# Joining C and V in one transpose, diagonal blocks of old states, and a new order of the tensor engine's groups in a chunked linear-attention kernel with a routed MLP behind it

## The chip, the cores and the metric

The kernel runs on one core of one Trainium2 chip. The metric is the device time of one execution in microseconds (us). Profiles and traces come from the hardware profiler on that core; in them PE is the tensor engine's matmuls, PEld its weight loads, DVE the vector engine, ACT the scalar engine, POOL GpSimd and SP the engine that issues most of the transfers. "Ln" is line n of the kernel.

## The reference

Two blocks, one behind the other. The first runs, for each of 4 x 8 heads, a 40 x 40 state over 768 time steps; the second sends each token to one of eight experts (by a hash of its id) and applies a two-layer MLP.

```python
def _attn_ref(r, k, v, w, a, b):              # all (4, 8, 768, 40)
    state = zeros((B, H, D, D))
    for t in range(S):
        y[:, :, t] = einsum('bhd,bhde->bhe', rt, state)       # read with the state before t
        Sa = einsum('bhde,bhe->bhd', state, at)
        state = state * wt[:, :, None, :] - einsum('bhd,bhe->bhde', Sa, bt)
        state = state + einsum('bhd,bhe->bhde', vt, kt)
    return y

def _moe_ref(x, token_ids, w1, w2):           # x = y as (3072, 320)
    expert_idx = token_ids * 2654435761 % 8
    for e in range(8):
        xe = x[expert_idx == e]
        out[expert_idx == e] = maximum(xe @ w1[e], 0) @ w2[e]  # 320 -> 1024 -> 320
```

Everything is float32. The change touches the first block alone.

## The kernel before

The time axis is cut into 12 chunks of C = 64 steps; D = 40, R = C + D = 104. A **tile** u is one chunk of two of the four batches (NG = 2 groups of batches), so there are 24 tiles of 16 heads. A head is named by `be` (batch of the two), `hp` (pair of heads, 0..3) and `par` (which head of the pair); `al = hp // 2`, `hq = hp % 2`. A pair's two heads lie in columns 0..39 and 64..103 of a 104-wide row; after a transpose they lie in partitions 0..39 and 64..103, which is what `half40(par)` selects.

The work is written as steps, each with a time in **ticks**; the program sorts all steps by that time and emits them in that order, so each engine runs them in that order. Tile u has its transposes of `at` and `z` and its scores `a` in tick u, and its recurrent part in tick u + 8. A tick thus holds the first part of one tile and the recurrent part of the one eight before it: ticks 0 to 7 have only first parts, ticks 24 to 32 only recurrent parts. Within a tick the order is that of `STEPS`:

```python
    psa = apool("psa", 2, space=bass.MemoryType.PSUM)      # single banks: bank(...)
    psb = apool("psb", 3, space=bass.MemoryType.PSUM)      # pairs of banks: two_banks(...)
    st_r = ring("st", NG, [R, 2, HP, D], all_of)           # states
    sd_r = ring("sd", NG, [R, 2, HP, D], all_of)           # old states, transposed
    ...
    STEPS = ["r1", "v_t", "at_t", "c", "z", "x", "y", "r_t", "sd", "s", "a", "r0", "u", "rc"]
```

The recurrent part of tile u, with t0 = u + 8 (`mm` is one matmul, `heads_by` yields the heads in the order named):

```python
        @at_tick(t0 - 1, "v_t")                        # V transposed, half the partitions at a time
        def _():
            p = two_banks("v_ps")
            for hp in range(HP):
                for be in range(2):
                    rows = half(1 - be)
                    nc.tensor.transpose(p[0:R, be, hp * C:(hp + 1) * C], x["x"][rows, be, hp, 0:R], ident[rows, rows])
            nc.scalar.copy(t[0:R].rearrange("p b h t -> p b (h t)"), p[0:R, :, 0:HP * C])

        @at_tick(t0 - 1, "r0")                         # r1, part from the state: a matmul per head
        def _():
            x["r1_ps"] = p = two_banks("r1_ps")
            for par, be, hp in heads_by("hq", "be", "al", "par"):
                c0 = (hp % HQ * 2 + be) * D
                mm(p[half(al(hp)), par, c0:c0 + D], x["at_t"][half40(par), hp, be, :], st[half40(par), be, hp, :], ...)

        @at_tick(t0, "r1")                             # r1, part from V; 8 matmuls, then a copy
        ...
        @at_tick(t0, "c")                              # C (for the state) and C transposed (for the scores)
        def _():
            p = two_banks("c_ps")
            for par, be, hp in heads_by("hq", "be", "al", "par"):
                mm(p[half(par), a, c0:c0 + C], r1[half(a), par, hp % HQ * 2 + be, :], um[half(a), h, :])
            if not last:
                q = two_banks("nc_ps")
                for par, be, hp in heads_by("hq", "par", "al", "be"):
                    mm(q[half(be), a, c0:c0 + D], um[half(a), h, :], r1[half(a), par, hp % HQ * 2 + be, 0:D])
            nc.scalar.copy(ct[:]..., p...)             # c_t
            ...                                        # two copies of q into x["x"], beside V

        @at_tick(t0, "rc")                             # scores of r: with C and with V, a matmul each
        def _():
            p = two_banks("rc_ps")
            for i in range(2):
                for par, be, hp in heads_by("hq", "al", "be", "par"):
                    c0 = (hp * 2 + be) * C
                    mm(p[half(be ^ i), par, c0:c0 + C], x["v_t" if i else "c_t"][half40(par), be, hp, :],
                       x["r_t"][half40(par), hp, be, :])
            nc.vector.tensor_tensor(mr..., p..., after..., op=OP.mult)      # mask, 128 x 1024

            @at_tick(t0, "s")                          # new state
            def _():
                p = bank([P, 2, HP * D], "s_ps")
                mm(p[0:R], ident[0:R, 0:R], flat, stop=False)               # the old state, 320 columns
                for par, be, hp in heads_by("be", "al", "hq", "par"):
                    mm(p[half40(par), be, hp * D:(hp + 1) * D], x["z"][:, be, hp, cols], x["x"][:, be, hp, cols], ...)
                for be in range(2):                    # times the decay of the chunk, 104 x 160 each
                    nc.vector.tensor_tensor(st[:, be], p[0:R, be]..., pend, op=OP.mult)

        @at_tick(t0 + 1, "y")                          # output rows: r times old state, scores times z
        def _():
            p = two_banks("y_ps")
            for par, be, hp in heads_by("al", "hq", "be", "par"):
                mm(p[half(be), par, hp * D:(hp + 1) * D], x["r_t"][half40(par), hp, be, :], sd[half40(par), be, hp, :], ...)
            for par, be, hp in heads_by("al", "hq", "par", "be"):
                mm(p[half(be), par, hp * D:(hp + 1) * D], x["mr"][:, par, hp * 2 + be, :], x["z"][...], start=False)
            nc.vector.tensor_tensor(by_parity(xs), p..., by_parity(x["py"]), op=OP.mult)

            @at_tick(t0 + 1, "sd")                     # 8 transposes of the state, two copies of 40 x 320
```

Beside these, a tick holds the transposes `at_t` (4), `z` (8) and `r_t` (4), the scores `a` (32 matmuls), and the steps `x` and `u` (16 matmuls each, 32 x 32 x 32) that finish a 64 x 64 triangular inverse; groups of four tiles have 32-step inverses on the vector engine (`outer`, `ub`), and six rounds of running products of the decays w lie there too (`pb`, `qb`). Behind the last tick comes the MLP.

Of the kernel before, what the change touches and what calls it, by code (L numbers as in the profile page):

```python
# [33 lines left out]
F32 = mybir.dt.float32  # L34
# [9 lines left out]
def kernel(  # L44
# [102 lines left out]
    psa = apool("psa", 2, space=bass.MemoryType.PSUM)  # L147
    psb = apool("psb", 3, space=bass.MemoryType.PSUM)
# [31 lines left out]
    st_r = ring("st", NG, [R, 2, HP, D], all_of)  # L180
    sd_r = ring("sd", NG, [R, 2, HP, D], all_of)
# [51 lines left out]
    def heads_by(*order):  # L233

        sizes = {"par": 2, "be": 2, "al": 2, "hq": HQ}
        idx = [{}]
        for o in order:
            idx = [{**d, o: i} for d in idx for i in range(sizes[o])]
        for d in idx:
            yield d["par"], d.get("be"), d["al"] * HQ + d["hq"]  # L240
# [37 lines left out]
    STEPS = ["r1", "v_t", "at_t", "c", "z", "x", "y", "r_t", "sd", "s", "a", "r0", "u", "rc"]  # L278
# [111 lines left out]
    def tile_a(u):  # L390
# [20 lines left out]
        @at_tick(u - 0.5)  # L411
# [25 lines left out]
        def _():  # L437
            gi, ti = divmod(u, GRP)
            p = two_banks("a_ps")
            for kb in range(2):  # L440
                order = ("hq", "al", "be", "par") if kb == 0 else ("hq", "be", "al", "par")
                for par, be, hp in heads_by(*order):

                    i, c0 = (1 - be, hp * C) if kb == 0 else (al(hp), (HP + be * HQ + hp % HQ) * C)
                    mm(p[half(i), par, c0:c0 + C], x["z_t"][half40(par), be, hp, half(be if kb else 1 - be)],
                       x["at_t"][half40(par), hp, be, :])
# [65 lines left out]
    def tile_m(u, t0):  # L512
# [6 lines left out]
        def _():  # L519
# [3 lines left out]
            for par, be, hp in heads_by(*x_order):  # L523
# [10 lines left out]
        def _():  # L534
            ug, xi = groups[gi]["ug"][:, ti * H:(ti + 1) * H, :], x["xi"]
            p = bank([P, H, BLK], "u_ps")
            for par, be, hp in heads_by(*x_order):
# [5 lines left out]
    def tile_s(u, t0):  # L543
# [24 lines left out]
        @at_tick(t0 - 1, "v_t")  # L568
        def _():
            x["v_t"] = t = work.tile([P, 2, HP, C], F32, tag="v_t", name="v_t")  # L570
            p = two_banks("v_ps")
            for hp in range(HP):
                for be in range(2):
                    rows = half(1 - be)
                    nc.tensor.transpose(p[0:R, be, hp * C:(hp + 1) * C], x["x"][rows, be, hp, 0:R], ident[rows, rows])
            nc.scalar.copy(t[0:R].rearrange("p b h t -> p b (h t)"), p[0:R, :, 0:HP * C])

    def tile_b(u, t0):
# [6 lines left out]
        def _():  # L585
            x["r1_ps"] = p = two_banks("r1_ps")
            for par, be, hp in heads_by("hq", "be", "al", "par"):
                c0 = (hp % HQ * 2 + be) * D
                mm(p[half(al(hp)), par, c0:c0 + D], x["at_t"][half40(par), hp, be, :], st[half40(par), be, hp, :],
                   start=be == 0 and hp % HQ == 0, stop=False)  # L590

        @at_tick(t0, "r1")
        def _():
            p = x.pop("r1_ps")

            for par, _, hp in heads_by("hq", "par", "al"):
                c0 = hp % HQ * 2 * D
                mm(p[half(al(hp)), par, c0:c0 + 2 * D], x["mk"][:, par, hp, :], x["x"][:, :, hp, par * C:par * C + D],
                   start=False)
            x["r1"] = r1 = r1_r(u)  # L600
            nc.scalar.copy(r1[:, :, :, 0:D], p[:, :, 0:HP * D].rearrange("p two (x e) -> p two x e", e=D))

        @at_tick(t0, "c")
        def _():

            r1, um = x["r1"], x["um"]
            p = two_banks("c_ps")
            for par, be, hp in heads_by("hq", "be", "al", "par"):
                h, a = hx(par, be, hp), al(hp)
                c0 = (be * HQ + hp % HQ) * C  # L610
                mm(p[half(par), a, c0:c0 + C], r1[half(a), par, hp % HQ * 2 + be, :], um[half(a), h, :])
            if not last:
                q = two_banks("nc_ps")
                for par, be, hp in heads_by("hq", "par", "al", "be"):
                    h, a = hx(par, be, hp), al(hp)
                    c0 = (hp % HQ * 2 + par) * D
                    mm(q[half(be), a, c0:c0 + D], um[half(a), h, :], r1[half(a), par, hp % HQ * 2 + be, 0:D])
            x["c_t"] = ct = work.tile([P, 2, HP, C], F32, tag="c_t", name="c_t", bufs=1)
            nc.scalar.copy(ct[:].rearrange("p b (a q) t -> p a b (q t)", a=2),
                           p[:, :, 0:HP * C].rearrange("p a (b x) -> p a b x", b=2))  # L620
            if not last:
                for be in range(2):
                    nc.scalar.copy(x["x"][half(be), be].rearrange("p (a q) (two e) -> p a (q two) e", a=2, two=2)[:, :, :, 0:D],
                                   q[half(be), :, 0:HP * D].rearrange("p a (x e) -> p a x e", e=D))

        @at_tick(t0, "rc")
        def _():
            p = two_banks("rc_ps")
            for i in range(2):
                for par, be, hp in heads_by("hq", "al", "be", "par"):  # L630

                    c0 = (hp * 2 + be) * C
                    mm(p[half(be ^ i), par, c0:c0 + C], x["v_t" if i else "c_t"][half40(par), be, hp, :],
                       x["r_t"][half40(par), hp, be, :])
# [5 lines left out]
        if not last:  # L640
            @at_tick(t0, "s")
            def _():
                p = bank([P, 2, HP * D], "s_ps")
                flat = st[:].rearrange("p b h e -> p b (h e)")
                mm(p[0:R], ident[0:R, 0:R], flat, stop=False)
                for par, be, hp in heads_by("be", "al", "hq", "par"):
# [5 lines left out]
                for be in range(2):  # L652
                    pend = pend_r(ri)[:, :, rn, 2 * g + be].unsqueeze(2).to_broadcast([R, HP, D])
# [451 lines left out]
```

## Time and profile before

| | us |
|---|---|
| median of three runs | 780.6 (779.1 to 787.19) |
| span of the profiled execution | 790.1 |
| PE / PEld / DVE / ACT / POOL busy | 640.8 / 473.6 / 375.8 / 267.2 / 227.9 |
| scores of r masked (`mr`) of the first / last tile start at | 145.48 / 504.90 |

Busy time of an engine is the sum of its instructions' spans. On PE these overlap in the pipeline and end by a model, so the time of a group of matmuls is better read as the distance between the starts of that group and of the next. Every float32 matmul stands in the trace as two records (two pairs of a weight load and a matmul), every transpose as one. The 24 starts of `mr` cut the attention block into tiles: one per tick. A timeline line has start, length, engine, line, operation, output tile and input tiles, sizes (partitions x columns of the weights, then partitions x elements of the output), how many instructions were merged, and in brackets the idle time of the engine before it and what ended it; "issue" there means that nothing in the trace explains the wait.

### The profile page before, as it was taken

The numbers are of one execution on the slowest core, as the hardware profiler recorded it, in microseconds if no ns is written. First come the engines' busy times: TensorE is split into PE (matmuls) and PEld (weight loads), VectorE is DVE, ScalarE is ACT, GpSimd is POOL, SyncE is SP. The second block draws the span as 40 slices with busy tenths as digits, with TensorE's granted clock in tenths as the row PEclk, the third lists the DMA queues.
The fourth block names the chain that finished last, engine by engine and source line by source line (L and its number), as shares of the span: only waits on it lengthen the run. The fifth ranks groups of instructions, "written<-read, shape, count | busy, mean of one in ns | idle before, by whom it ended". The sixth has DMA issues, their size and how long they took to land.

```text
span 790.1 us, 25829 instructions
## 1 busy us (share of the span) xinstructions
PE 640.8 (81%) x11272; PEld 473.6 (60%) x11272; DVE 375.8 (48%) x925; ACT 267.2 (34%) x598; POOL 227.9 (29%) x383
## 2 busy tenths in 40 slices
PE   0055558888888888787888989679999999999995
PEld 0044446767777777676777877536555565564653
DVE  8155999956765887455647733222202022020210
ACT  0023335534454555364554545200213032100110
POOL 3223214313253633433341312161231312312101
PEclk9999999957887988789897979869999999999998
DMA  4979884864698688586252332382435327323000
GB/s 89 176 134 168 145 140 102 158 121 80 90 144 132 107 130 136 80 162 97 37 70 64 69 78 54 75 280 89 139 101 159 100 92 249 84 84 101 25 9 19
DMA packets 205686, 86.35 MB, mean 109 GB/s; under 512 B 186687, under 2 KB 196160, under 8 KB 205569
## 3 DMA queue, kind: packets, MB, share of 16 engines
q1 hardware_dynamic: 193408, 47.60, 33.1%
q0 software_dynamic: 12160, 37.06, 19.0%
q8 instruction: 89, 1.46, 0.8%
q14 instruction: 29, 0.23, 0.1%
HBM read 68.85 MB, written 16.42 MB: 108 GB/s over the span
## 4 chain that ended last, share of the span: by engine, by line
PE 50%; issue 24%; DVE 12%; DMA 4%; POOL 4%; SPq 3%; ACT 1%; POOLq 0%; DVEq 0%; another core or an unknown queue 0%
PE y_ps L252 6%; PE up_ps L887 6%; PE dn_ps L905 5%; PE s_ps L252 4%; PE t_ps L467 4%; PE r_ps L252 4%; PE rc_ps L252 3%; PE z_ps L432 3%; PE sd_ps L683 3%; PE x_ps L252 2%; DMA qb<-in_w_dram 2%; PE c_ps L252 2%; PE a_ps L252 2%; POOL out_dram L910 2%; PE nc_ps L252 2%
## 5 line engine op out<-in xcount | busy, mean ns | idle before, releaser
L895 DVE TENSOR_SCALAR ht<-up_ps 128x448 f32<-128x448 f32 x32 | 20.0, 625 | 196.4 <-PE up_ps L892 130.5
L905 PE MATMUL dn_ps<-w,ht 128*128 128x320 f32 (+1 forms) x448 | 109.5, 433 | 0.0
L905 PEld LDWEIGHTS dn_ps<-w,ht 128*128 128x128 f32 (+1 forms) x448 | 72.0, 177 | 32.1 <-issue 1.3
L887 PE MATMUL up_ps<-xt,w 128*128 128x448 f32 x224 | 87.5, 544 | 0.0
L910 POOL DMA_INDIRECT out_dram<-o,idx_all x28 | 27.6, 986 | 196.4 <-ACT o L909 191.4
L675 POOL DMA_DIRECT2D x_rows<-xs x44 | 23.3, 535 | 200.0 <-DVE xs L669 163.2
L887 PEld LDWEIGHTS up_ps<-xt,w 128*128 128x128 f32 x224 | 41.7, 190 | 43.1 <-issue 37.9
L501 DVE TENSOR_TENSOR ub<-ub,outer 128x31 f32<-128x31 f32 (+15 forms) x186 | 63.8, 343 | 6.4
L498 DVE TENSOR_TENSOR outer<-ub,nb 128x31 f32<-128x31 f32 (+15 forms) x186 | 63.0, 339 | 4.8
L897 ACT ACTIVATE ht<-up_ps 128x448 f32<-128x448 f32 x32 | 17.4, 543 | 130.5 <-PE up_ps L892 102.2
L909 ACT COPY o<-dn_ps 128x320 f32<-128x320 f32 x28 | 11.9, 425 | 103.3 <-PE dn_ps L905 103.3
L404 POOL DMA_DIRECT2D pl<-p_rows x48 | 25.9, 539 | 67.9 <-DVE at L417 52.6
L669 DVE TENSOR_TENSOR xs<-y_ps,py 128x320 f32<-128x320 f32 x24 | 11.8, 491 | 67.0 <-PE y_ps L252 66.8
L252 PE MATMUL a_ps<-at_t,z_t 40*64 40x64 f32 x1536 | 38.9, 256 | 4.8 <-ACT z_t L434 4.7
L344 PE MATMUL f_ps<-own,partner 128*128 128x40 f32 x12 | 3.7, 393 | 47.5 <-DVE own L339 46.9
L252 PEld LDWEIGHTS a_ps<-at_t,z_t 40*64 40x64 f32 x1536 | 33.8, 163 | 10.3 <-ACT z_t L434 9.0
L432 PE MATMUL z_ps<-ident,z 128*104 128x128 f32 x192 | 38.5, 366 | 1.9 <-DVE mr L636 1.1
L467 PE MATMUL t_ps<-ident,at 128*104 128x128 f32 x96 | 24.0, 399 | 16.4 <-DVE at L417 14.3
L252 PE MATMUL y_ps<-z,mr 128*64 128x40 f32 x768 | 33.2, 250 | 2.8 <-issue 1.9
L636 DVE TENSOR_TENSOR mr<-rc_ps,after 128x1024 f32<-128x1024 f32 x24 | 29.1, 1214 | 11.3 <-PE rc_ps L252 11.2
L432 PEld LDWEIGHTS z_ps<-ident,z 128*104 128x104 f32 x192 | 31.6, 178 | 3.8 <-issue 1.3
L861 POOL DMA_INDIRECT xg<-x_rows,src_all x28 | 27.0, 963 | 20.9 <-DVE selq L1002 12.7
(180 smaller groups left out, 1247.5 us busy)
## 6 DMA issues: line engine op xcount, KB each, us to landing
ql<-q_rows POOLq DMA_DIRECT2D x48, 160.0 KB
w<-in_moe_w_dram SPq DMA_DIRECT2D x10, 640.0 KB
w<-in_moe_w_dram SPq DMA_DIRECT2D x10, 512.0 KB
qb<-in_w_dram SPq DMA_DIRECT2D x24, 160.0 KB
al<-in_a_dram SPq DMA_DIRECT2D x48, 80.0 KB
kb<-in_b_dram SPq DMA_DIRECT2D x48, 80.0 KB
kb<-in_k_dram SPq DMA_DIRECT2D x48, 80.0 KB
p_rows<-pb SPq DMA_DIRECT2D x24, 160.0 KB
```

Source lines behind the costliest of these rows:

```text
L252: nc.tensor.matmul(out_, lhsT=lhsT, rhs=rhs, start=start, stop=stop, skip_group_check=True)
L404: nc.gpsimd.dma_start(pl[half(be)], of_batches(p_rows, 2 * g + be, 1))
L432: nc.tensor.transpose(p[0:R, be, hp * P:(hp + 1) * P], x["z"][:, be, hp, :], ident[:])
L467: nc.tensor.transpose(p[0:R, hp, :], src[:, hp, 0:R], ident[:])
L498: nc.vector.tensor_tensor(tv, ub[:, 0:j + 1, j:j + 1].to_broadcast([P, j + 1, m]), nb[:, j, j + 1:].unsqueeze(1).to_broadcast([P, j + 1, m ...
L501: nc.vector.tensor_tensor(o, o, tv, op=OP.add)
L636: nc.vector.tensor_tensor(t[:].rearrange("p two h t -> p (two h) t"), p[:].rearrange("p two (h t) -> p (two h) t", t=C), after[:].unsqueez ...
L683: nc.tensor.transpose(p[0:D, be, hp * R:(hp + 1) * R], st[:, be, hp, :], ident[0:R, 0:R])
L861: nc.gpsimd.indirect_dma_start(out=xg[0:m], out_offset=None, in_=x_rows[:], in_offset=bass.IndirectOffsetOnAxis(ap=idx, axis=0))
L887: nc.tensor.matmul(p[:], lhsT=w1[c][:, (f0 + i) * P:(f0 + i + 1) * P], rhs=xt[:, c, 0:n], start=(c == 0), stop=False)
L905: nc.tensor.matmul(p[i * m:(i + 1) * m], lhsT=ht[:, f, c0:c0 + m], rhs=w2[f // (FP // 2)][:, f % (FP // 2), :], start=(f == 0), stop=(f == ...
L910: st = nc.gpsimd.indirect_dma_start(out=out[:], out_offset=bass.IndirectOffsetOnAxis(ap=idx, axis=0), in_=o[0:m], in_offset=None, bounds_c ...
```

## The change

C (the result of the triangular solve) is no longer computed a second time in transposed form. `nc` writes it beside V in `x`, and one 128-row transpose `x_t` of C and V together gives the operand for the scores of r, which then need one matmul per head with 128 columns of weights where there were two with 64. The old states are kept as 104 x 104 blocks with the two heads of a pair on the diagonal and zeros elsewhere, so `r0` and the first half of `y` take one matmul with 104 rows per pair of heads where there was one with 40 rows per head, and their results (and `y`) fit in single PSUM banks. PSUM is dealt out anew: four single banks and two pairs, where there were two and three. The steps of a tick are put in a new order, in which groups of many short matmuls stand in turn with groups of few long ones.

```diff
-    psa = apool("psa", 2, space=bass.MemoryType.PSUM)
-    psb = apool("psb", 3, space=bass.MemoryType.PSUM)
+    psa = apool("psa", 4, space=bass.MemoryType.PSUM)
+    psb = apool("psb", 2, space=bass.MemoryType.PSUM)
-    st_r = ring("st", NG, [R, 2, HP, D], all_of)
-    sd_r = ring("sd", NG, [R, 2, HP, D], all_of)
+    st_r = ring("st", NG, [R, 2, HP, R], all_of)
+    sd_r = ring("sd", NG, [R, 2, HP, 2, D], all_of)
-    STEPS = ["r1", "v_t", "at_t", "c", "z", "x", "y", "r_t", "sd", "s", "a", "r0", "u", "rc"]
+    STEPS = ["r1", "r0", "z", "nc", "y", "at_t", "x", "x_t", "s", "u", "r_t", "sd", "a", "rc"]
-        @at_tick(u - 0.5)                      # vector engine: at and z of the tile
+        @at_tick(u - 0.6)
-        @at_tick(t0 - 1, "v_t")                # whole step removed: 8 transposes, one copy
...
         @at_tick(t0 - 1, "r0")
-            x["r1_ps"] = p = two_banks("r1_ps")
-            for par, be, hp in heads_by("hq", "be", "al", "par"):
-                mm(p[half(al(hp)), par, c0:c0 + D], x["at_t"][half40(par), hp, be, :], st[half40(par), be, hp, :],
+            x["r1_ps"] = p = bank([P, DM], "r1_ps").rearrange("p (two x e) -> p two x e", two=2, e=D)
+            for _, be, hp in heads_of("hq", "be", "al"):
+                mm(p[half(al(hp)), :, hp % HQ * 2 + be, :], x["at_t"][0:R, hp, be, :], heads(st[:, be, hp]),
...
-        @at_tick(t0, "c")                      # the 16 matmuls into c_ps and the copy to c_t are removed
+        @at_tick(t0, "nc")                     # the 16 into nc_ps and its two copies stay, for the last chunk too
+        @at_tick(t0, "x_t")
+            x["x_t"] = t = work.tile([P, 2, HP, P], F32, tag="x_t", name="x_t", bufs=1)
+            p = two_banks("x_t_ps")
+            for be in range(2):
+                for hp in range(HP):
+                    nc.tensor.transpose(p[0:R, be, hp * P:(hp + 1) * P], x["x"][:, be, hp, 0:R], ident[:])
+            for be in range(2):
+                nc.scalar.copy(t[0:R, be].rearrange("p h t -> p (h t)"), p[0:R, be])
...
         @at_tick(t0, "rc")
-            for i in range(2):
-                for par, be, hp in heads_by("hq", "al", "be", "par"):
-                    mm(p[half(be ^ i), par, c0:c0 + C], x["v_t" if i else "c_t"][half40(par), be, hp, :],
-                       x["r_t"][half40(par), hp, be, :])
+            for par, be, hp in heads_of("be", "hp", "par"):
+                mm(p[:, par, c0:c0 + C], x["x_t"][half40(par), be, hp, :], x["r_t"][half40(par), hp, be, :])
...
             @at_tick(t0, "s")
-                mm(p[0:R], ident[0:R, 0:R], flat, stop=False)
+                for par in range(2):
+                    mm(p[half40(par)], ident[0:R, cols], st[:, :, :, cols], stop=False)
...
-                for be in range(2):            # 104 x 160, twice
-                    nc.vector.tensor_tensor(st[:, be], p[0:R, be]..., pend, op=OP.mult)
+                for par in range(2):           # 40 x 320, twice
+                    nc.vector.tensor_tensor(st[rows, :, :, par * C:par * C + D], p[rows]..., pend..., op=OP.mult)
...
         @at_tick(t0 + 1, "y")
-            p = two_banks("y_ps")
-            for par, be, hp in heads_by("al", "hq", "be", "par"):
-                mm(p[half(be), par, hp * D:(hp + 1) * D], x["r_t"][half40(par), hp, be, :], sd[half40(par), be, hp, :],
+            p = bank([P, DM], "y_ps")
+            for _, be, hp in heads_of("hp", "be"):
+                mm(p[half(be), c0:c0 + 2 * D], x["r_t"][0:R, hp, be, :], sd[:, be, hp].rearrange("p two e -> p (two e)"),
...
             @at_tick(t0 + 1, "sd")             # transposes of 104 x 104, two copies of 104 x 320
-                        nc.tensor.transpose(p[0:D, be, hp * R:(hp + 1) * R], st[:, be, hp, :], ident[0:R, 0:R])
+                        nc.tensor.transpose(p[0:R, be, hp * R:(hp + 1) * R], st[:, be, hp, :], ident[0:R, 0:R])
```

## The prediction, made before the change was run

> **What bounds the kernel now.** I read the page first, for the shares of the engines and the clock.
>
> ```profile
> span 790.1 us, 25829 instructions
> PE 640.8 (81%) x11272; PEld 473.6 (60%) x11272; DVE 375.8 (48%) x925; ACT 267.2 (34%) x598; POOL 227.9 (29%) x383
> ...
> PEclk9999999957887988789897979869999999999998
> DMA  4979884864698688586252332382435327323000
> ...
> q8 instruction: 89, 1.46, 0.8%
> ```
>
> PE leads, and its clock falls below full speed in slices 9 to 27 (19.75 us each, so 158 to 533 us): the attention block up to its end at 510 us and the first us of the MLP, which then runs at full clock and is not touched. The last line looks idle, but 89 packets of 16.4 KB are PE's program: 2 x 11272 instructions in blocks of 256 make 88. Next the engines in three parts of the block, cut at the starts of `mr` of tiles 0, 8, 15 and 23 (columns: PE, PEld, DVE, ACT, POOL busy, then clock, DMA share, GB/s):
>
> ```profile
> 145.50:293.90 148.40, 126.34 (x3489) 108.51 (x3489) 107.78 (x264) 75.22 (x178) 56.77 (x96) 0.78 0.71 116
> 293.90:417.60 123.70, 103.14 (x3020) 87.87 (x3020) 72.50 (x164) 63.90 (x146) 46.06 (x75) 0.86 0.62 96
> 417.60:504.90 87.30, 80.67 (x2636) 70.18 (x2636) 42.31 (x96) 43.11 (x98) 20.13 (x40) 0.87 0.29 64
> ```
>
> That is 18.6, 17.7 and 10.9 us per tile (8, 7 and 8 tiles). DVE needs 13.5, 10.4 and 5.3 of it. To see what PE needs without waits I take two undisturbed stretches of its timeline, and then a disturbed one:
>
> ```profile
> 266.13 0.68 PE L252 MATMUL y_ps<-sd,r_t 40*64 40x40 f32 x32
> 266.73 1.13 PE L252 MATMUL y_ps<-z,mr 128*64 128x40 f32 x32
> 267.80 0.65 PE L467 MATMUL t_ps<-ident,r 128*104 128x128 f32 x4
> 268.28 0.88 PE L683 MATMUL sd_ps<-ident,st 104*40 104x104 f32 x8
> 268.99 0.70 PE L252 MATMUL s_ps<-st,ident 104*104 104x320 f32 x2
> ...
> 270.37 1.16 PE L252 MATMUL a_ps<-at_t,z_t 40*64 40x64 f32 x64
> 271.35 0.63 PE L252 MATMUL r_ps<-st,at_t 40*64 40x40 f32 x32
> 271.91 0.69 PE L252 MATMUL u_ps<-ug,xi 32*32 32x32 f32 x32
> ...
> 327.59 0.64 PE L252 MATMUL rc_ps<-r_t,v_t 40*64 40x64 f32 x26
> 330.50 0.34 PE L252 MATMUL rc_ps<-r_t,v_t 40*64 40x64 f32 x6 [2.28 <-issue]
> ```
>
> Distances between starts give each group's time: y 0.60 + 1.07, r_t 0.48, sd 0.71, s 0.64 + 0.74, a 0.98, r0 0.56, u 0.62; the two halves of rc follow at 0.52 each (326 and 272 us). From other stretches come r1 0.72, v_t 0.60, at_t 0.5, c 0.65, nc 0.69, z 1.0, x 0.62. The sum is some 12.2 us for 434 records, against 18 us per tile. Short matmuls cost about 16 ns a record whatever they do (a: 0.98 / 64).
>
> So 6 us per tile are not work. The last line shows where: rc stops in the middle of its run, waiting for nothing. I set such gaps against the packets of the instruction queue in the trace. This gap ends at 330.50; a packet landed at 329.03. Of the 30 gaps of 0.5 us or more between 140 and 500 us, 23 end 1.3 to 1.8 us after a packet of that queue landed, and they lie whole numbers of blocks apart (a block is 128 pairs: the position of the gap within 128 records only drifts, from 84 down to 36, as waits and branches take places in the blocks too). The next packet then starts 1.0 to 5.4 us after PE goes on, 2.4 on average. A block is thus asked for when the one before it begins, and comes 2.4 + 1.1 (transfer) + 1.5 = **5.0 us** later, longer when the DMA queues are full. PE uses up 128 pairs of a, r0 and u in 2.2 us, and then stands. These 23 gaps sum to 38.7 us. They cost twice: the clock records show half clock for 17 stretches, 122 us in all, between 147 and 468 us, nearly all beginning within 3 us of such a gap.
>
> [...] The trace's half-clock stretches are 3.4 us or multiples of it[...]. [...]
>
> **The change part by part**, in records and us of PE per full tile:
> - v_t goes: -8, -0.60. c goes: -32, -0.65 (16 matmuls).
> - x_t comes: +8 transposes like z_t: +1.0.
> - rc: 64 records become 32, each with 128 columns of weights; two run beside each other where four did. Streamed columns per unit stay, so I keep 1.04 us: -32, 0.
> - r0: 32 become 16 of 104 x 64, 80 columns. r1 has such (16 in 0.72): -16, +0.16. First half of y the same: -16, 0.60 to 0.72, +0.12.
> - s: ident in two halves of 40 columns beside each other: +2, about 0. sd with wider weights: 0, +0.2.
>
> Sum: 434 - 94 = **340 records (-22%)**, and 12.2 + 0.2 = **12.4 us** of work. The work is the same; the gain can come only from gaps and clock. Blocks per tile fall from 3.39 to 2.66. At 5.0 us each, fetching needs 17.0 us before, which is near the measured 17.7 to 18.6, and 13.3 us after. The order helps as well: the tightest 128 pairs (end of s, u, r_t, sd, a) now take 3.3 us instead of 2.2.
>
> ACT: v_t's copy (0.59) and c_t's (0.59) go, two for x_t (1.18) come: 0. It does 75.22 / 8 = 9.4 us per tile, below PE. DVE: the two decay products have 320 instead of 160 elements per partition; 0.49 each by the row of `xs` (128x320, 0.491) instead of 0.315: +0.35 us per tile. PSUM: pairs of banks are taken by z, nc, x_t, sd, a, rc in turn, two buffers. z waits for the bank of a, and nc for that of rc, so for `mr`. The chain after a is: ACT copies 1.5, `mk` 0.69, about 0.6 of other DVE work, `mr` 1.22, hand-overs, some 4.4 us from the end of a. PE reaches nc after rc, r1, r0, z = 1.04 + 0.72 + 0.72 + 1.0 = 3.5 us. So I expect a new wait of up to 1 us at nc, in ticks with a.
>
> Per tile, then:
> - tiles 0 to 8, decays and inverses on DVE: 13.5 + 0.35 = 13.9 us of DVE, in order, with waits between: 16.0 instead of 18.6: 8 x 2.6 = 21 us.
> - tiles 8 to 15: fetch 13.3, PE 12.4 plus up to 1: 14.2 instead of 17.7: 7 x 3.5 = 24 us.
> - the last eight, without z, at_t and a (work 12.4 - 2.5 = 9.9; 264 records = 2.1 blocks): 10.3 instead of 10.9: 5 us.
>
> Together 50 us: 780.6 - 50 = **730.6 us**.
>
> **The rivals.** (1) *Only the work counts.* If gaps are a symptom of something else (DMA, semaphores), equal work and 0.2 us more per tile give 780 to 786. Against it: the regular spacing in records and the constant 1.3 to 1.8 us after a packet. (2) *The PSUM wait takes the gaps' place.* Two pair buffers instead of three: if nc waits 2 us for a late `mr` in each of 16 ticks, and these waits halve the clock as the gaps do, the gain falls to some 15 us: 765. For it: DVE runs in order and is 73% busy in the first part. Against it: z, r0 and r1 stand between rc and nc, as r1, v_t, at_t and c did. (3) *Gaps vanish altogether and the clock stays full.* Then tiles take PE's 12.4 plus half a us in the middle part, DVE's 14.5 in the first, and 10 at the end: savings of 33 + 33 + 7 = 73 us: 707. (4) *DMA becomes the bound*: its share 0.71 at 18.6 us means 13.2 us per tile at a full share; below 16 us it would be over 0.8 busy, and loads and fetches take longer. That holds the gain of the first part to about half: 740.
>
> **Range and chances.** (3) sets the low end, with a little for better hand-overs; (2) and (4) together the high end: 702 to 762. Slower by over 2% (796) would need new waits larger than all gaps removed. I give faster by over 2% (below 765) 0.88, within 2% 0.09, slower 0.03.
>
> **What would show it.** PE should count 11272 - 24 x 94 matmuls, and 64 more for nc in the last chunk, so 9080; the instruction queue 2 x 9080 / 256 = 71 packets. "issue" gaps on PE in the block should fall from 38 us to under 15, PEclk in the slices of the block should rise from about 0.83 to 0.9 or more, and group times should be as listed: x_t 1.0, r0 and y's first half 0.72, rc 1.04. Gaps at nc released by `mr` should be below 1 us. If the gaps stay as they were with fewer packets, the fetch theory is wrong; if rc takes twice its time, my account of pairs beside each other is; if DVE or the DMA shows in PE's waits, rival (2) or (4) has it.

## The result and the profile after

The changed kernel takes **742.7 us** (median of four runs, 740.8 to 745.0) against 782.3 us for the kernel before (mean of 779.1, 780.6 and 787.2 us; a fourth execution took 793.6): a ratio of **0.9495** (95% interval 0.9418 to 0.9573), some 40 us less. The prediction was 730.6 us, range 702 to 762.

The page after, in the lines that answer to those shown of before:

```profile
span 742.6 us, 21441 instructions
PE 612.6 (82%) x9076; PEld 458.2 (62%) x9076; DVE 383.7 (52%) x925; ACT 263.8 (36%) x602; POOL 229.0 (31%) x383
...
PEclk9998555899899889998999998699999999999998
...
q8 instruction: 72, 1.18, 0.7%
```

2196 matmul records are gone, and 17 of the 89 blocks of program. The clock row is at 8 or 9 from slice 8 (130 us) to the end of the block at 460 us. (The three 5s ahead of it are ticks in which PE waits for the vector engine: between 57 and 135 us the transposes of z for 15.4 us and `f_ps` for 8.2. Before's first clock record lies at 140 us and the row fills in 9 up to there, but its step a takes 2.46 us at 65.7 us and 1.16 us at 270.4, and its z takes 1.91 us at 68.97, where z in the changed kernel takes 1.93 us under a clock record of 0.50, at 83.15, and 1.08 under 1.00, at 276.09. So it was at half clock too.) The three parts of the block, cut at `mr` of tiles 0, 8, 15 and 23 again (columns: PE, PEld, DVE, ACT, POOL busy, clock, DMA share, GB/s):

```profile
147.20:275.90 128.70, 116.69 (x2722) 101.98 (x2722) 109.07 (x263) 73.03 (x176) 56.67 (x96) 0.91 0.77 134
275.90:379.80 103.90, 97.85 (x2434) 86.72 (x2432) 75.43 (x165) 63.53 (x149) 47.78 (x78) 0.95 0.73 117
379.80:457.10 77.30, 74.72 (x1878) 67.17 (x1876) 45.50 (x100) 42.97 (x102) 20.13 (x40) 1.00 0.33 73
```

That is 16.1, 14.8 and 9.7 us per tile (before: 18.6, 17.7, 10.9), at a clock of 0.91, 0.95 and 1.00 (before: 0.78, 0.86, 0.87). What lies ahead of the block and behind it is unchanged: `mr` of the first tile starts at 147.2 us (before 145.5), and from `mr` of the last to the end it is 285.5 us (before 285.2). The profiled execution of before was some 9 us slower than its median, so the traces differ by 47.5 us and the times by 40.

With the gaps of PE set against the packets of the instruction queue as in the prediction, now between the first and the last `mr`: gaps of 0.5 us or more that end 1.2 to 1.85 us after a block landed are 22 with 36.8 us before, and **7 with 9.8 us** after. Half clock falls from **122.9 us to 33.7 us**. One term went the other way:

```profile
397.18 2.00 PE L253 MATMUL rc_ps<-r_t,x_t 40*128 40x64 f32 x32
399.11 0.77 PE L253 MATMUL r_ps<-x,mk 128*64 128x80 f32 x16
399.71 0.72 PE L253 MATMUL r_ps<-st,at_t 104*64 104x80 f32 x16
400.41 0.68 PE L253 MATMUL nc_ps<-r,um 64*64 64x40 f32 x32
401.02 0.77 PE L253 MATMUL y_ps<-sd,r_t 104*64 104x80 f32 x16
```

From start to start, rc takes 1.93 us, 60 ns a record, where 64 records of it took 1.09 us before (at 272.53 and at 490.11 us; the prediction has 1.04). The groups with diagonal blocks are as expected or better: r0 0.70, first half of y 0.60.

### The profile page after: what moved, and what is told of

It reads as the page before. It is cut to its first block, busy times and chain, and to the rows that moved or that the text cites. A ratio compares the mean times of both kernels' runs of the same rounds, so it can differ in the third digit from the quotient of the medians.

```text
span 742.6 us, 21441 instructions
## 1 busy us (share of the span) xinstructions
PE 612.6 (82%) x9076; PEld 458.2 (62%) x9076; DVE 383.7 (52%) x925; ACT 263.8 (36%) x602; POOL 229.0 (31%) x383
## 4 chain that ended last, share of the span: by engine, by line
PE 42%; issue 21%; DVE 19%; DMA 6%; SPq 4%; POOL 4%; ACT 2%; POOLq 0%; DVEq 0%; ACTq 0%
PE up_ps L875 6%; PE dn_ps L893 6%; PE y_ps L253 4%; PE rc_ps L253 4%; DVE outer L499 3%; DVE ub L502 3%; PE s_ps L253 3%; DMA kb<-in_k_dram 3%; PE x_t_ps L612 3%; PE t_ps L468 2%; PE a_ps L253 2%; SPq L272 2%; PE r_ps L253 2%; POOL out_dram L898 2%; POOL xg L849 2%
## 5 line engine op out<-in xcount | busy, mean ns | idle before, releaser
L893 PEld LDWEIGHTS dn_ps<-w,ht 128*128 128x128 f32 (+1 forms) x448 | 72.0, 177 | 32.1 <-issue 1.3
L885 ACT ACTIVATE ht<-up_ps 128x448 f32<-128x448 f32 x32 | 17.4, 543 | 130.0 <-PE up_ps L880 130.0
L433 PE MATMUL z_ps<-ident,z 128*104 128x128 f32 x192 | 36.1, 348 | 21.8 <-DVE z L420 20.1
L253 PE MATMUL rc_ps<-r_t,x_t 40*128 40x64 f32 x768 | 49.9, 281 | 2.5 <-issue 1.8
L253 PEld LDWEIGHTS rc_ps<-r_t,x_t 40*128 40x128 f32 x768 | 46.4, 193 | 5.1 <-issue 1.9
L435 ACT COPY z_t<-z_ps 104x512 f32<-104x512 f32 x48 | 25.7, 588 | 64.0 <-PE z_ps L433 64.0
L433 PEld LDWEIGHTS z_ps<-ident,z 128*104 128x104 f32 x192 | 27.9, 166 | 25.8 <-issue 17.1
L253 PE MATMUL a_ps<-at_t,z_t 40*64 40x64 f32 x1536 | 32.7, 241 | 10.1 <-ACT at_t L469 6.1
L623 DVE TENSOR_TENSOR mr<-rc_ps,after 128x1024 f32<-128x1024 f32 x24 | 29.1, 1213 | 18.5 <-PE rc_ps L253 18.5
L253 PEld LDWEIGHTS a_ps<-at_t,z_t 40*64 40x64 f32 x1536 | 28.9, 152 | 15.6 <-ACT at_t L469 8.7
L345 PEld LDWEIGHTS f_ps<-own,partner 128*128 128x128 f32 x12 | 2.6, 271 | 52.2 <-DVE own L340 51.4
```

Of the source, the lines that this page charges most:

```text
L253: nc.tensor.matmul(out_, lhsT=lhsT, rhs=rhs, start=start, stop=stop, skip_group_check=True)
L433: nc.tensor.transpose(p[0:R, be, hp * P:(hp + 1) * P], x["z"][:, be, hp, :], ident[:])
L435: nc.scalar.copy(t[0:R, be].rearrange("p h t -> p (h t)"), p[0:R, be])
L623: nc.vector.tensor_tensor(t[:].rearrange("p two h t -> p (two h) t"), p[:].rearrange("p two (h t) -> p (two h) t", t=C), after[:].unsqueez ...
L893: nc.tensor.matmul(p[i * m:(i + 1) * m], lhsT=ht[:, f, c0:c0 + m], rhs=w2[f // (FP // 2)][:, f % (FP // 2), :], start=(f == 0), stop=(f == ...
```

## The experiments

Two theories stood after the result. **Fetch**: PE waits for its program, and half clock is what follows from those waits. **Activity**: the clock is halved by any stretch of some 3.4 us (the raster of the trace's clock records, 3.41 us) in which little work runs over all 128 rows of the array, whether PE waits in it or not. Both explain the gain of the whole change. They part where order and number of records are taken apart. What each run's profile shows, one row each (parts of the block in us per tile; fetch gaps and half clock between the first and the last `mr`, in us):

| kernel | median us | ratio to before (95%) | us per tile | fetch gaps | half clock |
|---|---|---|---|---|---|
| before | 783.9 | 1 | 18.5, 17.7, 10.9 | 36.8 | 122.9 |
| changed | 742.7 | 0.9495 (0.9418 to 0.9573) | 16.1, 14.8, 9.7 | 9.8 | 33.7 |
| o_new | 814.6 | none | 17.4, 19.0, 13.7 | 8.6 | 192.9 |
| o_old | 796.3 | 0.9993 (0.9771 to 1.0215) | 17.9, 19.2, 11.4 | 4.0 | 158.9 |
| d_many | 792.3 | 0.9952 (0.9921 to 0.9983) | 17.3, 18.1, 11.2 | 10.2 | 51.2 |
| d_few | 781.4 | 0.9846 (0.9752 to 0.994) | 16.8, 17.5, 11.3 | 1.6 | 37.5 |
| u_late | 757.5 | 0.9587 (0.9498 to 0.9676) | 15.6, 16.8, 9.7 | 3.6 | 61.4 |
| oold_d | 770.4 | 0.9743 (0.9631 to 0.9855) | 16.9, 15.4, 11.2 | 3.1 | 31.6 |
| bef_d | 789.8 | 0.9986 (0.9877 to 1.0095) | 19.7, 18.0, 10.4 | 19.4 | 95.6 |
| rc64 | 745.3 | 0.9458 (0.9372 to 0.9544) | 15.9, 15.4, 9.1 | 14.3 | 32.1 |
| xt_only | 798.3 | 1.029 (1.0131 to 1.045) | 18.7, 17.6, 12.5 | 10.9 | 176.7 |
| dg_only | 779.1 | 0.9998 (0.9942 to 1.0054) | 16.9, 16.7, 11.0 | 20.7 | 86.3 |
| a_early | 760.4 | 0.9818 (0.9696 to 0.9941) | 16.1, 16.1, 9.8 | 5.1 | 44.7 |
| a_early64 | 757.0 | 0.981 (0.9655 to 0.9965) | 16.2, 16.3, 9.7 | 16.0 | 51.1 |

The runs lie on several chips, and kernels that lose much clock scatter by 3% and more from execution to execution (`o_old` 774.6 to 802.5 us), so the ratio, taken against before on the same chip and from undisturbed runs, decides, and the profile of a single execution shows the kind of loss and not its last us.

### Order alone, and everything but the order

`o_new` is before with the new order, `o_old` the changed kernel with the old one.

```diff
# o_new, from before
-    STEPS = ["r1", "v_t", "at_t", "c", "z", "x", "y", "r_t", "sd", "s", "a", "r0", "u", "rc"]
+    STEPS = ["r1", "r0", "z", "c", "y", "at_t", "x", "v_t", "s", "u", "r_t", "sd", "a", "rc"]
-        @at_tick(u - 0.5)
+        @at_tick(u - 0.6)
# o_old, from the changed kernel
-    STEPS = ["r1", "r0", "z", "nc", "y", "at_t", "x", "x_t", "s", "u", "r_t", "sd", "a", "rc"]
+    STEPS = ["r1", "at_t", "nc", "z", "x", "y", "x_t", "r_t", "sd", "s", "a", "r0", "u", "rc"]
-        @at_tick(u - 0.6)
+        @at_tick(u - 0.5)
```

> The kernel before with nothing changed but the order of the steps in a tick (v_t in the place of x_t, c in that of nc). Fetch theory (PE waits for blocks of 256 instructions, and the half clock follows from these waits): still 434 records a tile, so still 3.4 blocks a tile and nearly the same fetching time, but no run of 128 short pairs in 2.2 us any more; the gaps fall from 38.7 us to some 20 and the time to 760 to 772 us. Rival, work and semaphores alone: no change, 778 to 785. Rival, the order is the whole gain: about 743.

> The changed kernel with the order of before (x_t just before r_t). Fetch theory: 340 records a tile, 2.7 blocks; a, r0 and u together are now 112 records in 2.4 us, so a few gaps come back: 745 to 757 us, gaps under 20 us. If the order were the whole gain, it would return to about 780. If the order gave nothing: 742.

`o_new` ran at 785 to 828 us where before ran at 777 to 803 on the same chip; no ratio can be given for it, but a gain it was not. The fetch gaps fell further than expected, to 8.6 us, and the time did not follow. `o_old` needs as few blocks as the changed kernel (72) and its fetch gaps are 4.0 us, yet its time is that of before. Both expectations fail, and the fetch theory with them as an account of the clock: with hardly a fetch gap, half clock is 193 and 159 us. (The few gaps may in part be a result of the half clock, at which PE uses up its program more slowly: z in the changed kernel took 1.93 us against 1.08. So these two runs don't show what order alone does to the gaps.) What the trace of `o_old` shows instead, first three windows of 3.4 us (columns as above), then PE's timeline over them:

```profile
463.10:466.50 3.40, 3.40 (x95) 2.88 (x93) 0.98 (x2) 2.02 (x5) 1.79 (x4) 1.00 0.59 122
466.50:469.90 3.40, 2.87 (x65) 2.60 (x58) 1.22 (x1) 1.15 (x3) 0.00 (x0) 1.00 0.34 56
469.90:473.30 3.40, 3.40 (x90) 3.26 (x90) 0.00 (x0) 2.21 (x6) 0.00 (x0) 0.50 0.02 5
```

```profile
466.57 2.00 PE L253 MATMUL rc_ps<-r_t,x_t 40*128 40x64 f32 x32
468.50 0.77 PE L253 MATMUL r_ps<-x,mk 128*64 128x80 f32 x16
469.80 1.04 PE L253 MATMUL nc_ps<-r,um 64*64 64x40 f32 x32 [0.53 <-ACT r L590]
470.78 1.06 PE L253 MATMUL x_ps<-ut,no 32*32 32x32 f32 x32
```

In the window before the clock drops, PE is busy for 2.87 of 3.40 us; its only gap is the 0.53 us wait for the copy of r1. But 1.93 us of that window are rc, whose weights are 40 rows deep.

So I tabulated all windows of 3.41 us (the raster of the clock records) that touch the block, over all fourteen kernels: how much of each window at full clock PE spent in groups with 104 or 128 rows (z, at_t, r_t, x_t, sd, s, r1, second half of y, and r0 and first half of y where they have diagonal blocks; and v_t, although it has 64), and whether the next window was at half clock:

| us with all rows in the window | windows | next at half clock |
|---|---|---|
| under 0.5 | 78 | 66 |
| 0.5 to 1.0 | 106 | 53 |
| 1.0 to 1.5 | 226 | 31 |
| 1.5 to 2.0 | 211 | 7 |
| over 2.0 | 454 | 0 |

The other way, out of half clock, 80 of 96 windows with over 3.0 us in such groups are followed by full clock, and none of 28 with under 1.0 us. `o_new` shows the way out: it falls to half clock less often than before (9 stretches against 17), but stays there for up to 85 us, and none of its 56 half-clock windows inside the block has over 3.0 us in such groups. Of the weights the rows tell more than the columns, and the length of the matmuls counts too: of the 1052 full-clock windows that lie whole in the block, 143 were followed by half clock. The 143 lowest by time in all-row groups (v_t left out) hold 99 of them, the 143 lowest by rows times streamed columns 118, by columns of the weights times streamed columns 75. Which measure the clock follows stays open. This is a count over traces, so it shows what goes together; the next runs test what causes what.

### Records and work set against each other

```diff
# d_many, from the changed kernel, ahead of step x's own matmuls
+            for i in range(47):
+                c0 = H * BLK + i // 2 % 8 * BLK
+                mm(pb[low(i % 2), c0:c0 + BLK], ident[top(i % 2), low(i % 2)], ident[top(i % 2), 0:BLK])
# d_few, in the same place
+            for i in range(4):
+                mm(pb[:, H * BLK:2 * H * BLK], ident[:], r256[:])
```

> The changed kernel with 47 matmuls of 32 x 32 x 32 more per tile behind step x (94 records, some 1.8 us of PE), into columns that nobody reads. Fetch theory: records are back at 434 a tile, so gaps of 25 us or more and the half clock come back, and the time is 785 to 805 us, clearly above the next run. Work theory: the same as the next run, 765 to 785.

> The changed kernel with 4 matmuls of 128 x 128 x 256 more per tile behind step x (8 records, some 1.7 us of PE), into columns that nobody reads. Fetch theory: blocks now last longer, so gaps vanish altogether (under 5 us) and the clock is full; PE work of 24 x 1.7 = 41 us is added, part of it in ticks that wait for the vector engine: 762 to 780 us, 15 us or more below the run with 94 short records. Work theory: equal to that run within 5 us.

(Both groups stand ahead of x's own matmuls, not behind them.) The added groups take 1.7 us per tile (94 short records) and 1.9 us (8 long ones) in the traces. The run with *more* work is faster: the four executions of `d_few` took 780.6 to 785.2 us, the twenty of `d_many` on the same chip 782.1 to 807.2. The intervals of the ratios, 0.9846 and 0.9952, overlap by a little; the ratios are 8 us apart where 15 were expected, and `d_few`, at 781.4 us, lies just above its 762 to 780. Fetch gaps are 10.2 us with 90 blocks and 1.6 us with 74, a difference of 8.6 us. The fetch theory thus stands for the gaps themselves. It was wrong in how many would come back: with the records at before's number, 10.2 us stood there and not 25 or more, probably because the groups lie better spread. The short records also have 32 rows, and half clock is 51 against 38 us, so a part of the distance can be activity; these two runs don't separate the parts.

### Work added to keep the clock

`oold_d` (from `o_old`) and `bef_d` (from before) add two matmuls over all rows to each tile, one ahead of u and one ahead of rc, in the long stretch without any. Their results are overwritten or not read.

```diff
-            p = bank([P, H, BLK], "u_ps")
+            pb = bank([P, 512], "u_ps")
+            mm(pb[:, 256:512], ident[:], r256[:])
+            p = pb[:, 0:256].rearrange("p (h t) -> p h t", h=H)
...
             p = two_banks("rc_ps")
+            mm(p[:, 0, 0:256], ident[:], r256[:])
```

> The changed kernel in the order of before, with one matmul of 128 x 128 x 256 more before u and one before rc (4 records and 0.86 us of PE work per tile, 20 us in all), into columns that are overwritten or not read. Activity theory: the long stretch with few rows is now broken by work on all rows, so half clock falls from 156 us to under 90 us and the time falls although work is added: 755 to 785, at least 10 us below the same order without them (796 median). Fetch theory or plain work: 20 us more, 805 to 817.

> The kernel before with the same two matmuls added per tile (one before u, one before rc; 20 us of PE work in all). Activity theory: half clock falls from 122 us to under 90 us, fetch gaps (38.7 us) shrink somewhat since the densest block now takes 3 us; time at or below that of before (770 to 795 where before has 780 to 795). Plain work: 20 us slower than before, 800 to 815.

`oold_d` is the cleanest answer of the study for the clock. The page's clock row of `o_old`, and then that of `oold_d`:

```profile
PEclk9995556799666797678669977869999999999998
```

```profile
PEclk9996555688999899899999999699999999999998
```

From 0.75 to 0.85 in the parts of the block the clock goes to 0.91, 0.97 and 1.00, half clock from 159 to 32 us, and the time falls to a ratio of 0.9743 (0.9631 to 0.9855) although every tile has over 1 us more to do:

```profile
458.31 0.70 PE L255 MATMUL u_ps<-r,ident 128*128 128x256 f32 x2
458.94 0.69 PE L255 MATMUL u_ps<-ug,xi 32*32 32x32 f32 x32
459.57 0.70 PE L255 MATMUL rc_ps<-r,ident 128*128 128x256 f32 x2
460.20 2.00 PE L255 MATMUL rc_ps<-r_t,x_t 40*128 40x64 f32 x32
```

Two useless matmuls of 0.63 us each (start to start) are repaid. Fetch can't be the reason: the fetch gaps were 4.0 us and are 3.1, and all waits of PE in the block together were 25.1 us and are 18.4. Nor is the trace an exception: the mean clock of a whole execution was 0.837 to 0.883 in the twenty of `o_old` and 0.909 to 0.916 in the four of `oold_d`. The two were timed on different chips, and the intervals of their ratios overlap between 0.977 and 0.986: the gain over before is shown, the gain in time over `o_old` is likely. `bef_d` shows the same in weaker form: 24 x 1.3 = 30 us of work added, and the ratio is 0.9986 (0.9877 to 1.0095). Plain work would have given 800 us and more. Its clock was 0.880 to 0.947 where before had 0.839 to 0.864 on the same chip; half clock fell to 95.6 us, not under 90 as expected.

`u_late` goes the other way: the changed kernel with u between a and rc.

```diff
-    STEPS = [..., "x_t", "s", "u", "r_t", "sd", "a", "rc"]
+    STEPS = [..., "x_t", "s", "r_t", "sd", "a", "u", "rc"]
```

> The changed kernel with step u moved from before r_t to between a and rc; nothing else. Then a, u and rc, which use 32 or 40 of the 128 rows of the array, stand together for 1.1 + 0.6 + 1.9 = 3.6 us. Activity theory (a stretch of some 3.4 us without matmuls over all rows halves the clock, whether PE waits or not): half clock in the block rises from 33 us to over 80 us and the time to 765 to 795 us, with fetch gaps still under 15 us. Fetch theory (half clock only follows gaps): r0 and rc keep the tightest block at over 3 us, so few new gaps, half clock under 50 us, time 740 to 752.

Half clock rises to 61 us with fewer fetch gaps than the changed kernel has, which is the sign that the activity theory asked for; its size is smaller than expected (80 us) and so is the loss: 757.5 us, 0.9587 (0.9498 to 0.9676). That interval overlaps the one of the changed kernel, so the loss of some 1% is likely and not shown. The mean clock of its four executions was 0.882 to 0.906, that of the changed kernel's four 0.909 to 0.916. Why the size is small is not shown.

### Each half of the change alone

`xt_only` is before with C and V joined and nothing else; `dg_only` is before with the diagonal blocks and nothing else. Both keep the old order and the old split of PSUM.

```diff
# xt_only, from before
-    STEPS = ["r1", "v_t", "at_t", "c", "z", "x", "y", "r_t", "sd", "s", "a", "r0", "u", "rc"]
+    STEPS = ["r1", "at_t", "nc", "z", "x", "y", "x_t", "r_t", "sd", "s", "a", "r0", "u", "rc"]
# steps v_t and c out; nc, x_t and rc as in the change
# dg_only, from before: st, sd, r0, r1, s, y and sd as in the change; v_t, c and rc as before
```

> The kernel before with the joining of C and V alone (v_t and c gone, x_t and the new rc in), states, banks and order as before (x_t just before r_t): 370 records a tile, 2.9 blocks. Activity theory: a, r0, u and rc, all with 32 or 40 rows, stand together for 4.1 us, longer than before since rc now takes 1.94 us, so half clock stays at 120 us or more although the fetch gaps fall below 25 us: 785 to 815 us, no gain. Fetch theory: fewer blocks, gaps and half clock fall together: 760 to 778.

> The kernel before with the diagonal blocks alone (r0 and the first half of y with 104 rows, single banks for r1 and y, the new s and sd), PSUM split and order as before: 404 records a tile, 3.2 blocks. Activity theory: r0 now works on 104 rows in the middle of the stretch a, r0, u, rc, so half clock falls below 110 us: 765 to 785. Fetch theory: gaps fall only with the blocks, by some 7%: 775 to 782 where before has 780.

The joining alone is **slower**: 1.029 (1.0131 to 1.045). It takes 11 blocks away and the fetch gaps fall to 10.9 us, and half clock rises to 177 us: a, r0, u and the new rc now stand together for 4.1 us with 32 or 40 rows. Here a busy PE loses its clock: it works through the whole of one window, from 271.40 us on with these four groups and 0.1 us of r1, and has half clock in the next (columns as above):

```profile
271.40:274.80 3.40, 3.40 (x126) 3.24 (x116) 2.11 (x6) 2.09 (x6) 3.17 (x6) 1.00 0.68 81
274.80:278.20 3.40, 3.40 (x54) 2.87 (x54) 3.19 (x6) 1.01 (x2) 1.17 (x3) 0.51 0.90 104
```

The diagonal blocks alone change nothing that can be measured: 0.9998 (0.9942 to 1.0054). Their half clock is lower (86 us) and gaps are fewer (20.7 us), but PE waits elsewhere: `u` follows `st` on the vector engine 9 times for 9.4 us in all. It waits for a bank: r0 now takes one of the two single banks, so u, two banks behind s, gets the one that `st` still reads. (In one tick r0 starts at 294.21 us, while `st` runs from 293.96 to 294.95, and u at 295.10.) The changed kernel has four single banks. The expected 765 to 785 us holds in number; the gain that it stood for does not show. So neither half brings the gain, nor does the new order without them: only both halves in the new order do, with the new split of PSUM, which was not tried by itself.

### The dear term, and what holds the tiles now

```diff
# rc64, from the changed kernel
-            for par, be, hp in heads_of("be", "hp", "par"):
-                c0 = (hp * 2 + be) * C
-                mm(p[:, par, c0:c0 + C], x["x_t"][half40(par), be, hp, :], x["r_t"][half40(par), hp, be, :])
+            for be in range(2):
+                for hp in range(HP):
+                    c0 = (hp * 2 + be) * C
+                    for i in range(2):
+                        for par in range(2):
+                            mm(p[half(i), par, c0:c0 + C], x["x_t"][half40(par), be, hp, half(i)], x["r_t"][half40(par), hp, be, :])
```

> The changed kernel with each matmul of rc cut into two halves of 64 columns of weights (64 records instead of 32 per tile, four tiles of the array in turn). If matmuls with 128 columns of weights don't run beside each other in two row groups (60 ns a record in the changed kernel) and four quarter tiles do (16 ns a record in the kernel before): rc falls from 1.94 to 1.05 us per tile, the last eight tiles from 9.7 to 8.9 us, and the time to 722 to 733 us; the 32 more records bring back a few us of fetch gaps. If the time of rc is that of its data and not of its form: no change, 740 to 745, or slower with the records.

```profile
399.31 1.16 PE L253 MATMUL rc_ps<-r_t,x_t 40*64 40x64 f32 x64
400.40 0.78 PE L253 MATMUL r_ps<-x,mk 128*64 128x80 f32 x16
```

rc falls from 1.93 to 1.09 us with twice the records, as foreseen, and the last eight tiles from 9.7 to 9.1 us. The total doesn't move: 0.9458 (0.9372 to 0.9544) against 0.9495 for the changed kernel. The trace shows the difference record by record. With 128 columns of weights two matmuls start 7 ns apart, and the next two come 112 ns after them; with 64 columns four start 7 ns apart each, and the next four come 58 ns after them, in `rc64` as in before (medians at full clock). Each streams 64 columns in either form. In the full ticks the 0.84 us are handed to other waits (who waited for whom, us in total, times, longest, from tile 0 to 15):

```profile
PE rc_ps L253 <- issue: 8.5, 13, 1.9
PE r_ps L253 <- issue: 4.3, 6, 1.4
PE nc_ps L253 <- DVE mr L626: 4.2, 5, 1.3
PE nc_ps L253 <- DVE outer L499: 3.2, 3, 1.7
PE z_ps L433 <- DVE mk L461: 2.8, 3, 1.4
```

In the changed kernel the same span has 1.8 us of rc behind issue, 5.8 us of nc behind the vector engine, and no z behind `mk` among its larger waits. The larger part thus goes to issue (rc and r1 have 12.8 us of it against 2.2), with fetch gaps up from 9.8 to 14.3 us. The rest goes to the vector engine (nc and z, 10.2 us against 5.8): to that extent the dear rc had been covering the time in which the masks `mk` and `mr` free their banks.

`a_early` tried to take that wait away by moving a ahead of s, so that the two masks no longer follow each other; `a_early64` does it with rc in halves.

```diff
-    STEPS = [..., "x_t", "s", "u", "r_t", "sd", "a", "rc"]
+    STEPS = [..., "x_t", "a", "s", "u", "r_t", "sd", "rc"]
```

> The changed kernel with step a moved between x_t and s. Then every group with few rows (nc, x, a, u, rc) has one with all rows on both sides, and the masks of a and rc no longer come one behind the other on the vector engine just ahead of z and nc. Activity and PSUM theory: half clock at or under 33 us, no PE waits for mk and mr: 728 to 741 us. If neither matters at this level: 742 to 745.

> The same, with rc in halves of 64 columns too. In the changed kernel's order the halves saved 0.9 us of PE per tile and the time stayed, since z and nc then waited for mk and mr and fetch gaps came back. Without those waits the saving should show: 715 to 732 us. If the vector engine holds the tile rate in itself: 738 to 745, as without the halves.

Both miss: 0.9818 and 0.981, slower than the changed kernel. `mk` is out of the way, but nc now waits 12.4 us for `mr`, in 8 waits. The vector engine of `a_early`:

```profile
306.15 1.98 DVE L510 STREAM_TRANSPOSE ut<-ub 128x1024 f32<-128x1024 f32 x1
308.00 1.90 DVE L511 STREAM_TRANSPOSE ug<-ub 128x1024 f32<-128x1024 f32 x1
309.93 1.22 DVE L623 TENSOR_TENSOR mr<-rc_ps,after 128x1024 f32<-128x1024 f32 x1
```

The times of the inverses are tied to the place of a in the tick (`t_a` in the kernel), so with a they moved ahead as well, and in one tick of four the two transposes of 1.9 us that end an inverse now stand ahead of `mr` instead of behind it. That the order of the vector engine is the whole reason is read from the trace; the version with a moved and the inverses left in place was not run. No version beat the changed kernel by more than the noise.

## Why the prediction was right, and where it was not

- **Records and blocks**: predicted 9080 and 71, measured 9076 and 72.
- **Fetch gaps** under 15 us: 9.8 us. Right, and d_few against d_many supports it.
- **Time per tile** 16.0, 14.2 and 10.3 us: 16.1, 14.8 and 9.7. The 23 tiles add up to 309.8 us predicted and 309.9 measured. That so exact a sum came out is luck: the middle part was too low by 4 us, the last too high by 5, and two terms behind it were wrong (below).
- **The miss of 12 us** in the total comes from the last subtraction. The 50 us saved were read from the trace of an execution of 790.1 us and taken from the median of 780.6. From the trace's own span the same 50 us give 740.1; 742.6 was measured.
- **The step that failed** in the sum of PE's work is in the sentence "two run beside each other where four did. Streamed columns per unit stay, so I keep 1.04 us". Two do run beside each other, 7 ns apart. But a unit's time did not stay with its 64 streamed columns: it was 58 ns with 64 columns of weights and 112 ns with 128, and rc took 1.93 us. The sum of PE's work is therefore some 13.0 us per tile and not 12.4. The 24 x 0.84 = 20 us don't show in the sum of the tiles. The middle part, 4 us over, may hold some of them; in the last eight tiles PE waits for only 2.6 us and the last two ticks take 9.0 and 7.3 us. Where the rest went is not shown; `rc64` takes the 0.84 us back and gains nothing.
- **"They cost twice"**: the prediction took half clock for a consequence of the fetch gaps. In the kernel before, both fall together, since PE stood still in the very stretch that had few rows. But o_old has half clock without fetch gaps, and oold_d takes it away by adding work. The loss to be removed was right in size, its cause was not, and the same edit happened to remove it. Between the first and the last `mr`, the waits of PE fell from 49.2 to 20.6 us and its busy time from 310.2 to 289.3. The 27 us less of fetch gaps are nearly all of the first. In the second, 89 us less half clock are worth some 35 to 43 us (an estimate: in the trace of before the same groups take 1.64 to 1.94 times as long under a clock record of 0.50 as under 1.00, v_t 0.36 us against 0.22 and sd 1.21 against 0.63, each from its first start to its last), and the dearer rc costs 20.
- **The order** was credited with the spacing of program blocks. It also spreads the groups over all rows, and that is what o_old (0.9993) lacks. It isn't enough by itself: o_new has it too, with r0 and the first half of y still on 40 rows, and lost the most clock.
- **The rivals**: (1), only the work counts, is refuted by d_few against d_many and by oold_d. (2), the PSUM wait takes the place of the gaps, is there in small: nc behind `mr` for 1.8 us, longest 0.9 (below 1 us was predicted), and behind `outer`, also on the vector engine, for 4.0 us, longest 1.8. (3), no gaps and full clock, did not come: 9.8 us of gaps and 33.7 us of half clock stayed. (4): the DMA share rose to 0.77 in the first part and no large wait of PE is put down to it.

## What to carry to other kernels

Read the granted clock beside the busy time: a tensor engine that is busy all the time can lose half its clock if its matmuls use few rows (xt_only at 271.40 us: busy for 3.40 of 3.40 us, and 0.51 of the clock in the next window), and then work over all rows inside the long stretch without any is worth more than fewer instructions, even if it is useless work (oold_d, 0.9743 of before). A new order alone did not do it (o_new). Count the records of a group and the columns of its weights as well as those that it streams (64 streamed columns took 58 ns with 64 columns of weights and 112 ns with 128), and where a run of 128 short pairs takes less than the trip of a program block (2.2 us against the prediction's estimate of 5.0), spread the short groups. Before a change that removes instructions is judged, try its order and its parts apart: here each alone gave nothing or a loss.

## What the runs showed of the hardware

- Clock: of 454 windows of 3.41 us at full clock with over 2 us of matmuls over 104 or 128 rows, none was followed by half clock; of 78 with under 0.5 us, 66 were. A window in which PE never waits can lose the clock (xt_only, 271.40 us: PE busy for 3.40 of 3.40 us, then a clock of 0.51). Windows with transposes lost it less often: of 82 windows with under 0.5 us of transposes and of other matmuls over all rows, 67 were followed by half clock; of 119 with as few matmuls but over 1.0 us of transposes, 7.
- Matmuls side by side: 40-row matmuls with 64 columns of weights, in turn over partitions 0..39 and 64..103 of the operands and both halves of the result's partitions, start four at a time, 7 ns apart, every 58 ns (64 streamed columns; before and rc64); with 128 columns of weights, in turn over partitions 0..39 and 64..103, they start two at a time every 112 ns (changed kernel).
- Program: the packets of the instruction queue have 16.4 KB each, and in the MLP (from 579.5 us before, from 533.6 after) they start 118 to 143 matmul records after one another, 128 and 127 on average, so some 256 instructions with the weight loads. The trip of a block, 5.0 us, is an estimate, worked out in the prediction from 2.4, 1.1 and 1.5 us in the trace of before. The first of these terms, from where PE goes on after a gap to the start of the next packet, was 2.8, 2.3 and 1.2 us in the three parts of the block, with a DMA share of 0.71, 0.62 and 0.29. The kernels with 72 to 78 packets in all have 1.6 to 16 us of fetch gaps in the block, those with 84 to 90 have 8.6 to 36.8. So the number of packets doesn't settle it: before, with 89, has 36.8, and d_many, with 90 and the short groups spread, 10.2.
